# An attention, feed-forward and soft-mixture kernel on one core: weight conversion without a clamp, its additions on VectorE, some low parts on TensorE, and a maximum's reader put last

## The chip, the cores and the metric

One core of a Trainium2 chip runs the whole program. The metric is the device time of one execution in microseconds, the median of the runs. Engines are named as in the profile: PE is TensorE's matmuls, PEld its weight loads, DVE VectorE, ACT ScalarE, POOL GpSimd, SP SyncE, which issues the transfers.

## The reference

Three stages follow each other, all in float32; the two weights of the middle one come as float64 (random values divided by a square root), the others as float32.

```python
for t in range(S):                                   # B, H, S, D = 4, 8, 768, 48
    cur = np.einsum('bhd,bhe->bhde', u[None] * kt, vt)
    y[:, :, t] = np.einsum('bhd,bhde->bhe', rt, state + cur)
    state = wt[:, :, :, None] * state + np.einsum('bhd,bhe->bhde', kt, vt)
...
h = x @ w_in                                         # 3072 x 384 by 384 x 2048
g = h * (1.0 / (1.0 + np.exp(-1.702 * h)))
x2 = g @ w_out                                       # 2048 x 384
...
logits = x2 @ phi                                    # 32 slots, 8 experts x 4
d = softmax of logits over the tokens; slot_input = d.T @ x2
slot_out[e] = np.maximum(slot_input[e] @ w1[e], 0) @ w2[e]      # F = 1024
out = (softmax of logits over the slots) @ slot_out
```

## The kernel before

**Work and tiles.** The 3072 tokens are six blocks u of 512, one for each 128 steps of the sequence; a block has four attention units of 128 tokens, one for each batch element b, so 24 units. A unit (`unit_nodes`, L519) works in two halves of 64 steps. VectorE forms the running products of the decay by two scans (`scan0` L552, `scan1` L566) with their ends between them (L557, L560), and multiplies r and k by them (`scale` L574). TensorE forms the products of k and r (`pa` L600) and turns k (`pk` L605); VectorE masks them (`msk` L612). TensorE then does half 0 and half 1 (`half` L652, L654), with VectorE's new state after each (`snew` L659). The bonus term, r times u times k summed over a head and multiplied by v, is formed beside it from a second copy of r, k and v in natural order, the tile `nat` (load L543): two multiplications (`ruk` L582, L583), a sum over each head (`qsum` L587), a multiplication of v by it (`qv` L590). `yev` (L662) adds both; TensorE turns the result (`xtr` L668), ScalarE takes the high part (`xhi` L679) and VectorE the low part (`xlo` L682) of the input of the next stage.

**The feed-forward stage** (`mm_nodes`, L730) needs its inputs as a high and a low fp32r part. For each block and each of 16 weight groups f it does nine matmuls of h (L746), two gelu evictions on ScalarE (L750, L754), their difference on VectorE (`glo` L758), and nine matmuls into x (L766 to L768). Block 1 is done in two halves of 256 tokens, the others in one of 512.

**The conversion of the weights** (`conv_nodes`, L468) happens once per group f while block 0 runs. A group is 128x768 float64 values, loaded as pairs of 32-bit words (L477). ScalarE takes the absolute value of the high words into `cq` (L482) and shifts the low words (L483); VectorE clamps (`c1a` L486), shifts and masks (`c1b` L490) and adds the sign (`c1c` L494); GpSimd or VectorE adds the shifted low words as integers (`c2` L498; all 16 on GpSimd before); ScalarE rounds to the high part (`c3` L501), and VectorE subtracts for the low part (`c4` L504). The clamp keeps exponents in a range that the shift can carry.

**The last stage** (`moe2_nodes`, L786 and on) accumulates logits and slot inputs block by block with a running maximum (L840, L836, L844, L848), and after block 5 does the experts (L1100, L1142) and the output (L1161, L1182).

**A check of the range** of the decay products is made near 500 us: `inside0` (L1018 to L1020) on VectorE forms a column of flags, `inside1` (L1023) reduces it over the partitions on GpSimd, `inside2` (L1027) reads the result on VectorE, and the last instructions of the program (L1030, L1206) branch to a general path (not taken here) by it.

**The order.** `Plan` (L67) is a list scheduler that runs when the kernel is built. Every step is a node with an engine (or a table of engines with a cost each, as `C2E`), an assumed cost, its needs, a priority `pr` and the buffers it takes. The plan walks through assumed time and gives each free engine the ready node of the lowest priority; the result is a fixed order on each engine, and an instruction that waits holds up all behind it on its engine. Priorities of the units, the conversion and the matmuls come from the constants `FIRST`, `PERIOD`, `CONV0`, `CONVD`, `ATT0`, `ATTD`; the first loads are ordered by `SOON`; `tend` is the assumed end of the matmuls of block 5. VectorE steps marked `port=True` and GpSimd steps are kept apart in the plan's time.

## Time and profile before

| what | value |
|---|---|
| median of 3 runs | 634.65 us (633.98 to 636.14) |
| the profiled execution | 633.73 us |
| its span in the trace | 631.9 us |
| granted clock of TensorE, mean | 0.99 |
| PE busy | 570.4 us, 90% of the span |
| VectorE busy | 431.6 us, 68% |
| ScalarE busy | 274.9 us, 44% |
| GpSimd busy | 90.3 us, 14% |

The profiled execution's time is 1.8 us above its span: what lies around the first and the last instruction. All sums are made against the profiled execution. The shares are of the whole span, and its stages have different limits: the first 66.8 us go by until the first matmul of h, the feed-forward stage runs to about 584 us, and the experts and the output follow.

### The profile page before, as it was taken

What the parts mean: (1) busy time and instruction counts of PE and PEld (TensorE: products, weight loads), DVE (VectorE), ACT (ScalarE), POOL (GpSimd) and SP (SyncE); (2) the same over time, 40 slices, a digit from 0 to 9 for tenths busy, and PEclk for the clock granted to TensorE, in tenths of its full rate; (3) what the DMA queues carried; (4) which work ended last, traced back from release to release, by engine and by line L of the source; (5) the groups of instructions that cost most, each with busy time, mean ns of one, the idle gap of its engine ahead of it and who ended that gap; (6) DMA issues with size and microseconds to landing.
All of it is one profiled execution on the core that took longest, in us unless ns stands there. A gap on an engine that the chain in (4) does not pass through costs nothing.

```text
span 631.9 us, 12380 instructions
## 1 busy us (share of the span) xinstructions
PE 570.4 (90%) x5092; PEld 462.7 (73%) x5092; DVE 431.6 (68%) x830; ACT 274.9 (44%) x524; POOL 90.3 (14%) x83
## 2 busy tenths in 40 slices
...
GB/s 294 233 240 209 140 104 158 215 150 76 115 114 114 107 108 113 7 107 74 91 76 101 55 110 77 101 113 28 74 39 1 95 357 147 153 229 249 306 152 219
DMA packets 29475, 86.08 MB, mean 136 GB/s; under 512 B 3040, under 2 KB 12384, under 8 KB 29408
## 3 DMA queue, kind: packets, MB, share of 16 engines
q1 hardware_dynamic: 29408, 85.19, 41.0%
...
HBM read 80.46 MB, written 4.72 MB: 135 GB/s over the span
## 4 chain that ended last, share of the span: by engine, by line
PE 74%; DVE 14%; issue 4%; DMA 3%; ACT 2%; POOL 1%; SPq 0%; ACTq 0%; DVEq 0%
PE h L746 28%; PE x L766 10%; PE x L767 9%; PE x L768 9%; PE y L652 5%; DMA raw<-in_wf_dram 2%; PE y L654 2%; PE aps L600 2%; PE so L1142 2%; PE eh L1100 2%; PE xps L668 1%; DVE glgh L758 1%; DVE at L574 1%; DVE at L552 1%; PE fo L1182 1%
## 5 line engine op out<-in xcount | busy, mean ns | idle before, releaser
L746 PE MATMUL h<-xth,w 128*128 128x512 f32 (+1 forms) x672 | 205.9, 371 | 3.2 <-ACT w L501 2.0
L750 ACT ACTIVATE ghgh<-h 128x512 fp32r<-128x512 f32 (+1 forms) x112 | 60.0, 537 | 231.7 <-PE h L746 171.0
L746 PEld LDWEIGHTS h<-xth,w 128*128 128x128 f32 x672 | 123.2, 191 | 25.8 <-ACT w L501 2.1
L766 PE MATMUL x<-ghgh,w 128*128 128x512 f32 (+1 forms) x336 | 125.7, 374 | 0.0
L746 PE MATMUL h<-xtl,w 128*128 128x512 f32 (+1 forms) x336 | 122.3, 364 | 0.5 <-DVE xtl L682 0.5
L767 PE MATMUL x<-glgh,w 128*128 128x512 f32 (+1 forms) x336 | 121.7, 362 | 0.6 <-DVE glgh L758 0.4
L768 PE MATMUL x<-ghgh,w 128*128 128x512 f32 (+1 forms) x336 | 121.4, 361 | 0.0
L758 DVE TENSOR_TENSOR glgh<-g,ghgh 128x512 fp32r<-128x512 f32 (+1 forms) x112 | 73.5, 657 | 55.4 <-ACT g L754 54.2
L766 PEld LDWEIGHTS x<-ghgh,w 128*128 128x128 f32 x336 | 63.9, 190 | 11.2 <-issue 0.6
L652 PEld LDWEIGHTS y<-vs,st 128*64 128x64 f32 (+2 forms) x768 | 55.0, 151 | 22.8 <-issue 13.2
L767 PEld LDWEIGHTS x<-glgh,w 128*128 128x128 f32 x336 | 63.9, 190 | 10.5 <-DVE glgh L758 1.9
L746 PEld LDWEIGHTS h<-xtl,w 128*128 128x128 f32 x336 | 64.2, 191 | 9.9 <-DVE xtl L682 1.4
L768 PEld LDWEIGHTS x<-ghgh,w 128*128 128x128 f32 x336 | 63.7, 190 | 9.6
L652 PE MATMUL y<-vs,st 128*64 128x48 f32 (+2 forms) x768 | 61.7, 238 | 9.0 <-DVE ind L551 4.7
L754 ACT ACTIVATE g<-h 128x512 f32<-128x512 f32 (+1 forms) x112 | 59.8, 534 | 4.8 <-DVE glgh L758 3.9
L654 PE MATMUL y<-vs,st 128*48 128x48 f32 (+2 forms) x704 | 50.1, 229 | 0.2 <-ACT st L622 0.2
L659 DVE TENSOR_TENSOR vs<-y,fl 48x384 f32<-48x384 f32 x44 | 24.4, 555 | 37.1 <-PE y L654 36.4
L498 POOL TENSOR_TENSOR cq<-cq,raw 128x768 int32<-128x768 int32 x16 | 32.1, 2008 | 112.2 <-DVE cq L494 52.2
L582 POOL TENSOR_TENSOR nat<-nat 128x384 f32<-128x384 f32 x16 | 16.2, 1012 | 217.4 <-DMA nat<-in_nat_dram 133.7
L654 PEld LDWEIGHTS y<-vs,st 128*48 128x48 f32 (+2 forms) x704 | 44.1, 133 | 0.8 <-ACT st L622 0.6
L600 PE MATMUL aps<-at 48*64 48x64 f32 x768 | 23.6, 239 | 20.5 <-DVE at L574 13.0
L612 DVE TENSOR_TENSOR st<-aps,mask 64x256 f32<-64x256 f32 (+1 forms) x80 | 37.8, 472 | 4.7 <-PE aps L600 3.7
(143 smaller groups left out, 695.8 us busy)
## 6 DMA issues: line engine op xcount, KB each, us to landing
...
```

The costliest lines, as they stand in the source:

```text
L498: onto[e].tensor_tensor(a, a, words(0), op=ALU.add)
L600: pe.matmul(ab[p if four else 0][vl:vh, col:col + CH], t_[a_][lo:hi, 1, 4 * g + h], t_[a_][lo:hi, 0, 4 * g + h], start=True, stop=True)
L612: ve.tensor_tensor(S[0][vl:vh, p, n * g:n * g + n, 0:CH], t_[kap[p if four else 0]][al:ah, 0:n * CH].rearrange("p (h t) -> p h t", h=n), m ...
L652: pe.matmul(yps[vl:vh, cols], S[0][0:k1, p, h, 0:CH], rhs, start=True, stop=True)
L654: pe.matmul(sps[ol:oh, cols], S[0][0:k1, p, h, CH:ROWS], rhs, start=True, stop=True)
L746: pe.matmul(h[:, :wd], a, b, start=(k == 0), stop=(k == len(seq) - 1))
L750: ac.activation(t_[kgh][0], t_[kh][:, :wd], AF.Gelu_apprx_sigmoid)
L754: ac.activation(t_[kg], t_[kh][:, :wd], AF.Gelu_apprx_sigmoid)
L758: ve.tensor_tensor(gl, t_[kg], gh.bitcast(F32), op=ALU.subtract)
L766: pe.matmul(o, whi, gh, start=(f == 0), stop=False)
L767: pe.matmul(o, whi, gl, start=False, stop=False)
L768: pe.matmul(o, wlo, gh, start=False, stop=(f == NF - 1))
```

## The change

- **Conversion.** The clamp `c1a` is gone. The absolute value is taken with a scale of 2 to the −112, which moves the exponent by itself, and ScalarE sums it into a column of `wchk` for each group; `inside0` tests the 16 sums in three more VectorE instructions. `c1b` only shifts.
- **Addition.** `C2E` names VectorE alone, so all 16 additions `c2` are VectorE's (L512 of the new kernel).
- **Low parts.** For groups 0 to 3 (`C4PE = 4`) the low part is formed on TensorE: for each half of 384 columns a product with the identity and one with its negative (`less`, made once on ScalarE) add up in a PSUM bank (L523, L524), and ScalarE copies the bank (L527).
- **Bonus sums of block 0** (`UQ = 1`). Its four units load only v in natural order. VectorE multiplies r and k in the transposed layout (`prk` L621), and 16 one-column matmuls with u as the moving column (`qpe` L627) sum them into free columns of the bank of `pk`; `qv` (L634) reads them there. u is loaded a second time, transposed, by two transfers (L474); its wide copy `ubt` is loaded later.
- **Order.** `SOON`, `FIRST`, `CONV0`, `CONVD` and `ATTD` change.
- **The reader.** GpSimd's all-reduce gets a priority of its own and a cost of 11.5, and its reader `inside2` (L1081) comes at `tend + 40`, after `nsi`.

```diff
-C2E = {"DVE": 1.16, "POOL": 1.95}
+C4PE = 4
+UQ = 1
+C2E = {"DVE": 0.96}
-SOON = "w0 r0 c0 n0 u w1 r1 v0 n1 v1 w2 r2 n2 v2 c1 w3 r3 n3 v3"
-FIRST, SECOND, PERIOD, LAG, AHEAD = 42.0, 150.0, 82.0, 4.2, 74.0
-CONV0, CONVD, CONVL = 0.0, 6.0, 16.0
-ATT0, ATTD = 3.0, 6.0
+SOON = "w0 r0 n0 c0 w1 r1 v0 n1 v1 w2 r2 n2 v2 c1 w3 r3 n3 v3"
+FIRST, SECOND, PERIOD, LAG, AHEAD = 30.0, 150.0, 82.0, 4.2, 74.0
+CONV0, CONVD, CONVL = 6.0, 5.0, 16.0
+ATT0, ATTD = 3.0, 3.0
...
+    def ld_u():
+        for lo, hi in ((CH, ROWS), (0, DH)):
+            sy.dma_start(ut[lo:hi], ub[0:1].rearrange("o (h d) -> d (o h)", h=NH))
...
-            ac.activation(t_[cq], words(1).bitcast(F32), AF.Abs)
+            ac.activation(t_[cq], words(1).bitcast(F32), AF.Abs, scale=2.0 ** -112, accum_out=wchk[:, f:f + 1])
...
-        def c1a():
-            ve.tensor_scalar(t_[cq], t_[cq], W_TINY, W_HUGE, op0=ALU.max, op1=ALU.min)
...
-            ve.tensor_scalar(a, a, 3, 0x3FFFFFF8, op0=ALU.logical_shift_left, op1=ALU.bitwise_and)
+            ve.tensor_scalar(a, a, 3, None, op0=ALU.logical_shift_left)
...
+        def c4p(z):
+            b, cols = bank(f"c4_{f}_{z}"), slice(z * DM, (z + 1) * DM)
+            pe.matmul(b[:, :DM], ident, t_[cq][:, cols], start=True, stop=False)
+            pe.matmul(b[:, :DM], t_["less"][:, 0, 0:P], wt[f][:, 0, cols], start=False, stop=True)
+        def c4a(z):
+            ac.activation(wt[f][:, 1, z * DM:(z + 1) * DM], t_[f"c4_{f}_{z}"][:, :DM], AF.Copy)
...
+            if few:
+                sy.dma_start(t_[n_][:, 2], nat[i, :, 2])
+            else:
+                sy.dma_start(t_[n_], nat[i])
...
+        def prk():
+            t = t_[a_][0:ROWS]
+            ve.tensor_tensor(rk(), t[:, 0], t[:, 1, :, ::-1], op=ALU.mult)
+        def qpe():
+            for h in range(NH):
+                for p in range(2):
+                    (lo, hi), (vl, vh) = RNG[p], VROW[p]
+                    pe.matmul(t_[kkp][vl:vh, 4 * ROWS + h:4 * ROWS + h + 1], rk()[lo:hi, h], ut[lo:hi, h:h + 1], start=True, stop=True)
...
+        ve.tensor_scalar(wchk, wchk, W_MOST, -1.0, op0=ALU.is_lt, op1=ALU.mult)
+        ve.tensor_reduce(t_["cm"][:, 2:3], wchk, axis=AX.X, op=ALU.max)
+        ve.tensor_tensor(t_["cm"][:, 0:1], t_["cm"][:, 0:1], t_["cm"][:, 2:3], op=ALU.max)
...
-    n = nin = N("DVE", 0.35, inside0, limits + [nep], tend - 70)
-    n = N("POOL", 0.57, inside1, [n], tend - 29)
-    nok = N("DVE", 0.1, inside2, [n], tend - 28)
+    n = nin = N("DVE", 0.75, inside0, limits + [nep], tend - 70)
+    nout = N("POOL", 11.5, inside1, [n], tend - 70)
...
+    nok = N("DVE", 0.1, inside2, [nout, nsi], tend + 40)
```

How the order of the instructions moves, at three places. The rows are those of the programs as built, in the order in which an engine takes them: line, operation, what it writes and reads, shape.

First, VectorE from the first `scale` (L574) of unit 0 on, before:

```order
L574 TENSOR_TENSOR at0_116<-at0_116 112x1024
L486 TENSOR_SCALAR cq0_140<-cq0_140 128x768
L490 TENSOR_SCALAR cq0_140<-cq0_140 128x768
L582 TENSOR_TENSOR nat0_133<-nat0_133 128x384
L583 TENSOR_TENSOR nat0_133<-nat0_133,ubt_90 128x384
L494 SCALAR_TENSOR_TENSOR cq0_140<-raw0_121,cq0_140 128x768
L612 TENSOR_TENSOR st0_96<-aps0_0_151,mask_79 64x8x64 x2
L587 TENSOR_REDUCE q0_209<-nat0_133 128x8
L590 TENSOR_TENSOR nat0_133<-nat0_133,q0_209 128x384
L659 TENSOR_TENSOR vs0_92<-y0_0_192,fl0_135 48x384
L551 MEMSET ind_91 112x8
L552 SCALAR_TENSOR_TENSOR at1_145<-at1_145,ind_91 112x512
```

and from the first `prk` (L621) of the changed kernel on, where `scale` is L604, the mask L656 and the scans L582 and L596:

```order
L621 TENSOR_TENSOR nat0_123<-at0_116 112x512
L504 TENSOR_SCALAR cq0_146<-cq0_146 128x768
L604 TENSOR_TENSOR at0_116<-at0_116 112x1024
L508 SCALAR_TENSOR_TENSOR cq0_146<-raw0_132,cq0_146 128x768
L581 MEMSET ind_91 112x8
L582 SCALAR_TENSOR_TENSOR at1_143<-at1_143,ind_91 112x512
L621 TENSOR_TENSOR nat1_151<-at1_143 112x512
L512 ISA cq0_146<-raw0_132,cq0_146 128x1536
L656 TENSOR_TENSOR st0_96<-aps0_0_165,mask_79 64x8x64
L587 TENSOR_TENSOR fl1_220<-at1_143 112x8
L656 TENSOR_TENSOR st0_96<-aps0_0_165,mask_79 64x8x64
L590 RECIPROCAL ind_91<-fl1_220 112x8
```

The clamp, the multiplications of `nat0` and the low part of group 0 are gone from this place; the scan of unit 1 and its `prk` stand before the masks of unit 0, and the addition (L512, 1536 elements in its listing) between them.

Second, TensorE between half 0 and half 1 of unit 0 (the results go to `y0_0`, the new state of half 1 to `y1_0`), before:

```order
L654 MATMUL y0_0_192<-vs0_92,st0_96 48x48
L652 MATMUL y0_0_192<-vs0_92,st0_96 64x48
L654 MATMUL y0_0_192<-vs0_92,st0_96 48x48
L652 MATMUL y0_0_192<-vs0_92,st0_96 64x48
L654 MATMUL y1_0_220<-vs0_92,st0_96 48x48
L652 MATMUL y0_0_192<-vs0_92,st0_96 64x48
L654 MATMUL y1_0_220<-vs0_92,st0_96 48x48
```

and now, where L696 and L698 are the matmuls of a half:

```order
L696 MATMUL y0_0_223<-vs0_92,st0_96 64x48
L698 MATMUL y0_0_223<-vs0_92,st0_96 48x48
L696 MATMUL y0_0_223<-vs0_92,st0_96 64x48
L698 MATMUL y0_0_223<-vs0_92,st0_96 48x48
L523 MATMUL c4_0_0_246<-cq0_146,ident_78 128x384
L524 MATMUL c4_0_0_246<-w0_145,less_121 128x384
L523 MATMUL c4_0_1_251<-cq0_146,ident_78 128x384
L524 MATMUL c4_0_1_251<-w0_145,less_121 128x384
L696 MATMUL y0_0_223<-vs0_92,st0_96 64x48
L698 MATMUL y1_0_263<-vs0_92,st0_96 48x48
L696 MATMUL y0_0_223<-vs0_92,st0_96 64x48
```

Before, half 1 followed half 0 directly; now the four products for the low part of group 0 (L523, L524) stand between them.

Third, VectorE at the check near 500 us, before, with the reader L1027 ahead of the running maximum (L840, L844) of block 4:

```order
L1018 MEMSET cm_5295 128x2
L1019 TENSOR_SCALAR rz_89<-rz_89 112x24
L1020 TENSOR_REDUCE cm_5295<-rz_89 112x1
L1027 TENSOR_SCALAR outside_5317<-cm_5295 128x1
L840 TENSOR_REDUCE mb4_5328<-lg4_5304 128x1
L844 TENSOR_SCALAR mrun0_83<-mb4_5328,mrun1_84 128x1
L819 COPY x2g_1405<-x2t4_0_5322 128x384
```

and now, where the maximum is L891 and L895:

```order
L1069 MEMSET cm_5363 128x3
L1070 TENSOR_SCALAR rz_89<-rz_89 112x24
L1071 TENSOR_REDUCE cm_5363<-rz_89 112x1
L1072 TENSOR_SCALAR mx_88<-mx_88 128x16
L1073 TENSOR_REDUCE cm_5363<-mx_88 128x1
L1074 TENSOR_TENSOR cm_5363<-cm_5363 128x1
L891 TENSOR_REDUCE mb4_5397<-lg4_5375 128x1
L895 TENSOR_SCALAR mrun0_83<-mb4_5397,mrun1_84 128x1
L870 COPY x2g_1313<-x2t4_0_5391 128x384
```

The reader, now L1081, is found after the slot inputs (L1059) and the first steps of block 5's softmax (L904, L905):

```order
L1059 TENSOR_TENSOR scrB_5370<-sp_5981,rz_89 128x24x4
L904 TENSOR_REDUCE rm5_5988<-ln5_5959 128x4
L905 TENSOR_TENSOR lc_1320<-ln5_5959,rm5_5988 128x128
L1081 TENSOR_SCALAR outside_6004<-cm_5363 128x1
L921 TENSOR_REDUCE zr5_6007<-lc_1320 128x4
```

The reader left the place directly behind the flags; three more instructions on flags (L1072 to L1074) stand there. On GpSimd the order of the all-reduce and its neighbours is the same in both.

## Rows read from the trace of the kernel before

**Rows 1.** The page: busy time of each engine, share of the span, instructions.
```profile
PE 570.4 (90%) x5092; PEld 462.7 (73%) x5092; DVE 431.6 (68%) x830; ACT 274.9 (44%) x524; POOL 90.3 (14%) x83
```

**Rows 2.** Windows: stretch, its length, busy PE, PEld, DVE, ACT, POOL, PEclk, DMA share, GB/s.
```profile
0.00:66.80 66.80, 31.11 (x412) 26.32 (x412) 61.70 (x105) 31.23 (x56) 13.77 (x16) 1.00 0.75 243
66.80:100.60 33.80, 33.76 (x135) 27.27 (x135) 28.32 (x38) 22.44 (x34) 9.43 (x5) 1.00 0.33 111
100.60:180.70 80.10, 74.07 (x794) 61.23 (x793) 71.83 (x125) 49.75 (x95) 17.85 (x13) 1.00 0.46 148
180.70:500.00 319.30, 318.17 (x2910) 264.41 (x2910) 238.88 (x488) 126.10 (x250) 47.00 (x45) 1.00 0.24 76
500.00:520.00 20.00, 15.14 (x89) 11.73 (x88) 6.61 (x21) 9.34 (x17) 1.78 (x5) 0.91 0.87 333
```

**Rows 3.** Waits of PE, 66.8 to 180.7: us in total, times, longest.
```profile
PE aps L600 <- ACT g L754: 2.6, 2, 1.4
PE h L746 <- ACT w L501: 2.0, 1, 2.0
```

**Rows 4.** Chain of waits, longest pieces: start, us, what.
```profile
66.84 9.39 PE h L746 x27
...
502.64 9.52 issue
```

**Rows 5.** Timeline, 500.9 to 514.8: start, us, engine, instruction, idle before it.
```profile
502.45 0.18 DVE L1020 TENSOR_REDUCE cm<-rz 112x1 f32<-112x24 f32 x1
...
507.76 0.82 PE L815 MATMUL x2t<-ident,x2t 128*128 128x128 f32 x6
512.16 0.38 POOL L1023 PARTITION_ALL_REDUCE cm<-cm  x1 [10.45 <-issue]
512.57 0.15 DVE L1027 TENSOR_SCALAR outside<-cm 128x1 int32<-128x1 f32 x1 [9.94 <-POOL cm L1023]
...
512.95 0.28 ACT L836 ACTIVATE lt<-lg 128x128 f32<-128x128 f32 x1 [7.58 <-DVE mb L840]
...
513.28 0.42 PE L848 MATMUL ln<-ident,lt 128*128 128x128 f32 x1 [4.71 <-ACT lt L836]
```

**Rows 6.** Lines of DVE, 0 to 160: form, count | busy, mean ns | idle before.
```profile
L494 DVE SCALAR_TENSOR_TENSOR cq<-raw,cq 128x768 int32<-128x768 int32 x16 | 15.2, 950 | 0.0
L504 DVE TENSOR_TENSOR w<-cq,w 128x768 fp32r<-128x768 f32 x16 | 15.1, 942 | 1.0 <-ACT w L501 1.0
L486 DVE TENSOR_SCALAR cq<-cq 128x768 f32<-128x768 f32 x16 | 13.4, 835 | 4.4 <-ACT cq L482 4.2
...
L574 DVE TENSOR_TENSOR at<-at 112x1024 f32<-112x1024 f32 x8 | 9.7, 1218 | 0.0
...
L612 DVE TENSOR_TENSOR st<-aps,mask 64x512 f32<-64x512 f32 x14 | 9.6, 685 | 2.7 <-PE aps L600 2.5
L490 DVE TENSOR_SCALAR cq<-cq 128x768 int32<-128x768 int32 x16 | 8.8, 553 | 0.0
...
L583 DVE TENSOR_TENSOR nat<-nat,ubt 128x384 f32<-128x384 f32 x8 | 6.0, 754 | 0.3
L590 DVE TENSOR_TENSOR nat<-nat,q 128x384 f32<-128x384 f32 x8 | 5.8, 723 | 0.1
...
L582 DVE TENSOR_TENSOR nat<-nat 128x384 f32<-128x384 f32 x8 | 4.3, 543 | 0.0
```

**Rows 7.** Line L498: count, ns least/median/most, first and last start.
```profile
L498 POOL TENSOR_TENSOR cq<-cq,raw x16: 1817/1914/2727, 14.7 to 147.1; 128x768 int32<-128x768 int32 x16
```

**Rows 8.** Timeline of DVE, 14.5 to 16, while L498 runs on POOL from 14.73.
```profile
15.04 1.93 DVE L590 TENSOR_TENSOR nat<-nat,q 128x384 f32<-128x384 f32 x1
```

**Rows 9.** Lines of PE, 600 to 632, shapes apart.
```profile
L1161 PE MATMUL ss<-sb,sel 128*128 128x192 f32 x8 | 1.8, 342 | 0.0
```

**Rows 10.** Line L679 on ACT: ns least/median/most.
```profile
L679 ACT ACTIVATE xth<-xps x24: 482/490/493, 22.6 to 500.2; 128x384 fp32r<-128x384 f32 x24
```

**Rows 11.** The page: DMA queue, packets, MB, share of 16 engines.
```profile
q1 hardware_dynamic: 29408, 85.19, 41.0%
```

More of the change, by code (lines that the diff above doesn't have):

```diff
@@ L456, in soon, with minus @@
         return keys.index(key) - 100.0 if key in keys else pr
-    lub = [N("DMA", 0.6, lambda: sy.dma_start(ubt, ub), pr=soon("u", 0.0))]
+    lub = [N("DMA", 0.6, lambda: sy.dma_start(ubt, ub), pr=30.0)]
     nst = [N("POOL", 1.49, lambda i=i: zeros(i), pr=-1 + i) for i in range(2)]
     nst += [N("ACT", 0.83, lambda i=i: eyes(i), [nst[i]], pr=-1 + i) for i in range(2)]
+    def minus():
+        t_["less"] = mp.tile([P, KC, T], F32R, tag="xtl", name="less", bufs=2)
+        ac.activation(t_["less"][:, 0, 0:P], ident, AF.Copy, scale=-1.0)
+    nless = N("ACT", act(P), minus, pr=5, take=[("xl", "less")])
+    def ld_u():
+        for lo, hi in ((CH, ROWS), (0, DH)):
+            sy.dma_start(ut[lo:hi], ub[0:1].rearrange("o (h d) -> d (o h)", h=NH))
+    lut = N("DMA", 0.3, ld_u, pr=-97.5)
     lphi = N("DMA", 0.2, lambda: sy.dma_start(phit, phi), pr=40)
@@ L512, in conv_nodes @@
         n = N("ACT", act(2 * DM), c3, [n], pr, use=[cq, wk])
-        conv[f] = N("DVE", dve(2 * DM), c4, [n], pr, use=[cq, wk], port=True)
+        if f < C4PE:
+            m = [N("PE", 1.3, lambda z=z: c4p(z), [n, nless], pr, take=[("ps", f"c4_{f}_{z}")], use=[cq, wk, "less"]) for z in range(2)]
+            m = [N("ACT", act(DM), lambda z=z: c4a(z), [m[z]], pr, use=[wk, f"c4_{f}_{z}"]) for z in range(2)]
+            conv[f] = N("X", 0.0, lambda: None, m, pr)
+        else:
+            conv[f] = N("DVE", dve(2 * DM), c4, [n], pr, use=[cq, wk], port=True)
     limits, grp_last = [], {}
@@ L688, in unit_nodes @@
         lv = N("DMA", 0.55, ld_v, [h.get("h0"), h.get("h1")], soon(f"v{i}", pr(2) - 6))
-        ln = N("DMA", 1.64, ld_n, pr=soon(f"n{i}", pr(1) - 5), take=[("nat", n_)])
+        few = u < UQ
+        ln = N("DMA", 0.55 if few else 1.64, ld_n, pr=soon(f"n{i}", pr(1) - 5), take=[("nat", n_)])
         def psum(key):
@@ L702, in unit_nodes @@
         rc = [N("ACT", act(512), lambda p=p: rcp(p), [r0, sd, kt.get((0, 1)) if p else None], pr(3.2 + p), use=[a_, s_]) if u or p else None for p in range(2)]
-        p0 = N(RUKE[u > 1], 0, ruk, [ln] + ([lub[0]] if i < 2 else []), pr(1.5), use=[n_], port=True)
+        if not few:
+            p0 = N(RUKE[u > 1], 0, ruk, [ln, lub[0]], pr(1.5), use=[n_], port=True)
         ta = N("PE", 0.8 if four else 1.08, pa, [a1, r0], pr(2), take=[x for k in kap for x in psum(k)], use=[a_])
@@ L712, in unit_nodes @@
         k1 = N("DVE", 2 * dve(256) if four else dve(512), lambda: msk(1), [ta, kt.get((1, 1))], pr(3.5), use=[kap[-1], s_])
-        qs = N("DVE", dve(DM), qsum, [p0], pr(3.6), take=[("q", q_)], use=[n_])
-        qm = N(QVE[u > 1], 0, qv, [qs], pr(3.8), use=[n_, q_], port=True)
+        if few:
+            qs = N("PE", 1.0, qpe, [tk, p0, lut], pr(3.2), use=[kkp, n_])
+            qm = N("DVE", dve(DM), lambda: qv("DVE"), [qs], pr(3.8), use=[n_, kkp])
+        else:
+            qs = N("DVE", dve(DM), qsum, [p0], pr(3.6), take=[("q", q_)], use=[n_])
+            qm = N(QVE[u > 1], 0, qv, [qs], pr(3.8), use=[n_, q_], port=True)
         h0 = N("PE", 1.06, lambda: half(0), [k0, rc[0], lv, h.get("s1")] + ke0, pr(4), take=psum(ky0), use=[s_])
```

18 lines of the change are left out of this document (11 added, 7 removed).

## The prediction

> **What bounds the kernel now.** I read the page first, then the windows, then the waits of one engine in one window, then the chain. The page gives one core, a span of 631.9 us and TensorE busy for 570.4 of it [rows 1]. That share is an average over stages with different limits, so the windows come next. Up to 66.8 us VectorE is busy for 61.70 and TensorE for 31.11: the head, which prepares block 0 and converts the first weights, is bound by VectorE. From 66.8 to 100.6 TensorE is full (33.76 of 33.80). From 100.6 to 180.7 it has 74.07 of 80.10, VectorE 71.83: the two share the limit. From 180.7 to 500 TensorE is full (318.17 of 319.30), and nothing that another engine saves there counts. From 500 to 520 there is a hole, 15.14 of 20, and the granted clock is 0.91 [rows 2].
>
> The waits tell what the idle time of 66.8 to 180.7 us is: TensorE waits 2.6 us for the gelu's eviction to free a bank, 2.0 for one converted weight (ScalarE's rounding at L501), and smaller things [rows 3]; the windows put all of it at 6.1. The chain gives the start of the first matmul of h, 66.84, and a piece of 9.52 us at 502.64 in which nothing is computed, which it calls issue [rows 4].
>
> That piece is the hole. VectorE's reduction (L1020) ends at 502.63, GpSimd's all-reduce (L1023) starts only at 512.16 and takes 0.38, and VectorE, whose next instruction reads its result (L1027), stands still for 9.94 us. Behind it in VectorE's order stands the maximum L840, ScalarE's L836 waits 7.58 for that, and TensorE waits 4.71 for ScalarE [rows 5].
>
> **The change, part by part.** The sum is made against the profiled execution, 633.73 us; the median of the runs, 634.65, is 0.9 above it.
>
> *Clamp, additions, low parts.* Per weight group VectorE loses the clamp L486 (0.835 us in the mean; its like without a neighbour on GpSimd, L490, takes 0.553) and gains the addition, which took GpSimd 1.914 in the median (L498) [rows 6, 7]. No row shows an integer addition on VectorE. The nearest is L494: the same 768 words of both operands, the same stride in the raw ones, 0.950. The other end follows from the order listing, where the instruction has 128x1536 elements, two for each word: L612 takes 0.685 for 512 elements and L574 1.218 for 1024, so 1.04 ns for each further one, and 1536 would take 1.75 [rows 6]. I take 0.95, since the traffic is that of L494 and since the planner's table, whose other entries stand near the rows (1.95 for the addition on GpSimd), has 0.96; 0.95 and 1.75 are the bounds.
>
> [...]
>
> Four groups lose the subtraction L504 on VectorE (0.942 each) [rows 6]. It becomes two products for each half on TensorE and a copy on ScalarE. An fp32 product of 192 columns takes 0.342 as recorded, ends included [rows 9]; 384 columns are then at most 0.7, an fp32r one of 384 at most the same: at most 2.8 us a group, 11 us in all, before the first h, in a stretch with 35 us of idle TensorE [rows 2]. So nothing, unless they stand in the way of a half. They stand between half 0 and half 1 of unit 0 (second order piece). They need the rounding on ScalarE, about 1 us after the addition; half 1 needs eight further VectorE rows, two masks of 0.685, a scan of 1.2 and others, some 4 us. The products fit between. The copies are 8 x 0.490, as L679 [rows 10], on ScalarE, which is busy for 31 of 66.8.
>
> *Block 0.* Each of its four units drops L582, L583 (0.543 and 0.754) and L587, of the same 384 elements and priced as L582, for one multiply of 112x512, priced as the mask L612 of 512, 0.685 [rows 6]. The sums become 16 one-column products a unit. Even at the 0.342 of 192 columns the 64 of them would be 22 us, which with the 11 above still fits into 35; I put nothing on them.
>
> *Up to the first h.* The order listings, cut at the low part of unit 3, give 6, 6, 6 and 5 instructions of L486, L490, L494 and L504 before, and 0, 5, 5 and 0 after. Undisturbed (L486 as L490, L583 as L582), the change takes away 6 x 0.553 + 0.553 + 0.950 + 5 x 0.942 + 4 x 3 x 0.543 = 16.0 us and adds 5 x 0.95 + 4 x 0.685 + 0.2 (one more reciprocal) = 7.7, so 8.3 less on the engine that bounds. GpSimd's additions, beside which an instruction of VectorE runs longer (one L590 took 1.93 where its mean is 0.723 [rows 6, 8]), are gone as well, some 2 us here. The bounds for the first h are therefore 0 and −10.3. I take **−5.5**, two thirds of 8.3: an engine that has less to do waits more, and it waits 5.1 us in this stretch already. The DMA order is the other reason: 384 KB less for each of the four units, but ahead of the first raw weights come two loads of u in pieces of 4 bytes, 768 of them. A packet takes 141 ns in the mean (41.0% of 16 engines' 631.9 us, over 29408) [rows 11], so at most 6.8 us over 16 engines, and nothing if pieces of 4 bytes are cheap. I put 0.5 on it, in the third that I leave out.
>
> *After the first h.* Over the 16 groups VectorE gets 16 x (0.95 − 0.835) = +1.8 for addition against clamp, less the disturbance of others (L583 and L590 by 8 x (0.754 − 0.543) and 8 x (0.723 − 0.543), 3.1 us). The supply of weights and the turns of VectorE make TensorE's 6.1 us of waits; they can go as a whole or not at all (0 and −6.1). VectorE has 13.8 us idle in these 114 already and gets some 1.3 more, and the weights arrive earlier; so I take **−4**.
>
> *The reader last.* The all-reduce stays where it is (third order piece), but VectorE's next is the maximum L840, now L891, which needs only logits that TensorE formed before the hole. The last thing TensorE does ahead of it ends at 508.58 [rows 5]; by then the maximum and ScalarE's L836 can be done. So the 4.71 us go, and a little of what the clock costs: 0.09 of 15.14 us is 1.4 at most. Bounds: −3.8 (if some other hand-off of 0.9, as ScalarE's after this one, is next) and −6.1. I take **−5.0**. What is late next would be the new reader, but it stands after all gelu work, some 60 us later, when the all-reduce is long done.
>
> *Added checks.* Three small VectorE instructions at 0.18 us at most, as L1020 [rows 5]: **+0.4**, and 16 reads of an accumulator on ScalarE beside other work.
>
> Sum: −5.5 − 4 − 5.0 + 0.4 = −14.1, so 633.7 − 14.1 = **619.6 us**.
>
> **The rivals.** *Dear addition (1.75 us).* Up to the first h five additions cost 4.0 more, leaving −1.5 of the first term; after it eleven cost 8.8 more, which eats the second term. With the hole gone: 633.7 − 1.5 − 5.0 + 0.4 = 627.6. For it: 1536 elements. Against: the traffic of L494. Chance 0.2.
>
> *The columns of u hold the head.* If the 4-byte pieces cost the 6.8 us of their upper bound ahead of the first raw weights, the first term becomes −5.5 + 6.3 = +0.8: 625.9. For it: DMA engines are 0.75 busy up to 66.8 [rows 2]. Against: 48 rows of 8 elements are little data. Chance 0.1.
>
> *The wait stays.* If something else in VectorE's or ScalarE's order still needs the all-reduce, or its start moves along, the third term is 0: 624.6. The order piece speaks against it. Chance 0.05.
>
> *Slower.* VectorE takes for the addition what GpSimd takes. L498 has 1.82 at the least and 2.73 at the most [rows 7]. With a price x, VectorE has 16 (x − 0.835) more, less 3.8 for L504, 4.6 for block 0 and 3.1 for disturbance; if nothing covers it, all of it falls on the time. With the 4.6 of the hole won, the kernel gets slower from x = 1.85; at 2.3 it is +11.9 − 4.6, that is 641. Against: every 768-element row of VectorE lies under 0.96 undisturbed, and VectorE still idles some 24 us up to 250. Chance 0.06.
>
> **How the numbers follow.** My forecast has 0.59. Its own range is 611 to 627: all bounds at their best give 633.7 − 10.3 − 6.1 − 6.1 + 0.4 = 611.6; at their worst, with a hole only partly filled, 630. The range to 629 takes in the first three rivals and leaves out the slower side and the unluckiest sums. A measurement of this kernel tells 0.3%, 1.9 us, from no change. Faster takes the forecast, the two rivals around 625 and most of the dear addition: 0.88. Same 0.06: the dear addition with nothing covered (VectorE then +3.1, the hole −4.6). Slower 0.06.
>
> **What would show it.** First h at about 61 us instead of 66.8; L512 of the new kernel at 0.95 us (1.75 shows the first rival, 1.9 and more the last); no instruction of 384 elements at 1.9; TensorE's idle time in the 114 us after it down from 6.1 to under 3; no wait of 9.9 us on VectorE near 500 and no stop of TensorE there; products of L523 and L524 inside TensorE's idle time. A first h that comes no earlier, with VectorE waiting for raw weights, shows the second rival. I am wrong if the first h comes earlier and the end does not: then TensorE, full from 180 us on, took the gain back in waits between.

## The result and the profile after

The changed kernel takes 614.57 us in the median (611.57 to 618.76, 4 runs) beside 635.39 for the kernel before on the same chip: a ratio of 0.9673, with a 95% interval of 0.9601 to 0.9745. A second set, listed below as `a_ctrl`, gives 615.37 (611.39 to 617.05, 6 runs) and 0.9669 (0.9626 to 0.9711). The profiled execution took 616.53, 17.2 us less than the 633.73 of before. That is near the forecast sum of −14.1, but the terms came out otherwise than their working had it.

The page of the changed kernel, busy time of each engine (before: [rows 1]):

```profile
PE 577.8 (94%) x5244; PEld 467.4 (76%) x5244; DVE 415.2 (68%) x822; ACT 279.5 (45%) x548; POOL 58.0 (9%) x67
```

Its windows, with the columns of [rows 2], cut at its own stages (63.5 is just ahead of its first matmul of h, 63.52):

```profile
0.00:63.50 63.50, 42.19 (x564) 32.87 (x565) 50.53 (x90) 32.52 (x65) 4.02 (x11) 0.84 0.68 210
63.50:93.00 29.50, 28.86 (x128) 23.66 (x127) 28.09 (x41) 24.07 (x43) 0.00 (x0) 1.00 0.54 173
93.00:140.00 47.00, 47.00 (x401) 38.17 (x400) 43.40 (x67) 32.57 (x60) 0.11 (x1) 1.00 0.47 150
140.00:190.00 50.00, 49.99 (x683) 46.74 (x681) 45.88 (x102) 26.57 (x63) 10.75 (x9) 1.00 0.44 140
190.00:487.00 297.00, 296.26 (x2637) 243.57 (x2636) 216.67 (x451) 118.78 (x230) 41.47 (x44) 1.00 0.24 74
487.00:505.00 18.00, 17.61 (x113) 13.40 (x112) 9.16 (x29) 10.98 (x20) 1.16 (x2) 1.00 0.97 371
```

Three things stand in them. The head, the stretch up to the first matmul of h, is 3.3 us shorter, and VectorE, busy for 61.70 of 66.80 before, is now busy for 50.53 of 63.50: it no longer bounds the head. TensorE is full from 93 us on, where 6.03 of 80.10 us were idle. And the hole near 500 us is gone, 17.61 of 18 where it was 15.14 of 20.

To say where time went, I cut each trace at TensorE's own landmarks: the first matmul of h, the 28th, the first of block 2, the first of block 5, the last, and the last matmul of the program. The 1008 matmuls of h are the same in all kernels. Work can stand on either side of a landmark: between the 27th and the 28th matmul of h before has two groups of nine matmuls into x, 4.3 us, and the changed kernel one, 2.3 us. So 2 us between the second and the third stretch are order; their sum compares. In us:

| stretch | before | after | difference |
|---|---|---|---|
| start to the first h | 66.84 | 63.52 | −3.3 |
| first 27 matmuls of h | 13.31 | 9.16 | −4.2 |
| to the first h of block 2 | 167.88 | 161.15 | −6.7 |
| blocks 2 to 4 | 254.01 | 253.87 | −0.1 |
| block 5 | 73.71 | 67.74 | −6.0 |
| last h to the last matmul | 44.94 | 48.00 | +3.1 |
| sum | 620.68 | 603.44 | −17.2 |

The third stretch is the change's largest gain, and the last a loss that the forecast did not have.

The price on which the first rival hung is in the lines of VectorE, 0 to 160 us (line, form, count | busy, mean ns | idle before):

```profile
L512 DVE CUSTOM_DVE_ANT_0 cq<-raw,cq 128x1536 uint16<-128x1536 uint16 x16 | 15.2, 953 | 0.1
L508 DVE SCALAR_TENSOR_TENSOR cq<-raw,cq 128x768 int32<-128x768 int32 x16 | 15.2, 950 | 0.1
```

The addition takes 0.953 us over 1536 two-byte elements, as its neighbour of 768 words does, and not the 1.75 of the other bound: 0.62 ns for an element, where each further element of L574 over L612 took 1.04 [rows 6]. A rule of the Trainium skill ("VectorE: DVE Perf Modes", section "Mode 2×_1P") lets two 2-byte values pass in a cycle where they are adjacent and aligned. Within each pair of the raw operand they are, and the 0.953 agrees with it; whether this custom instruction ran in that mode no run here shows.

The hole is closed in the way the forecast had it. The timeline of the changed kernel near 488 us; columns as in [rows 5]:

```profile
488.20 0.17 DVE L1072 TENSOR_SCALAR mx<-mx 128x16 f32<-128x16 f32 x1
488.39 0.17 DVE L1073 TENSOR_REDUCE cm<-mx 128x1 f32<-128x16 f32 x1
488.60 0.16 DVE L1074 TENSOR_TENSOR cm<-cm 128x1 f32<-128x1 f32 x1
...
490.75 0.29 DVE L891 TENSOR_REDUCE mb<-lg 128x1 f32<-128x128 f32 x1 [2.00 <-PE lg L884]
...
494.06 0.27 PE L899 MATMUL ln<-ident,lt 128*128 128x128 f32 x1
```

VectorE goes from the flags (three more instructions, 0.50 us) to the maximum, which waits for TensorE's logits alone. The transpose of the same logits (L899, before L848 with its 4.71 us of waiting) has no wait. The all-reduce itself still starts late, and its reader runs much later without a wait:

```profile
498.82 0.80 POOL L1077 PARTITION_ALL_REDUCE cm<-cm  x1 [11.46 <-DVE zr L923]
567.43 0.14 DVE L1081 TENSOR_SCALAR outside<-cm 128x1 int32<-128x1 f32 x1
```

### The profile page after: what moved, and what is told of

Its sections match the earlier page's. It is cut to its first block, busy times and chain, and to the rows that moved or that the text cites. A ratio compares the mean times of both kernels' runs of the same rounds, so it can differ in the third digit from the quotient of the medians.

```text
span 614.7 us, 12682 instructions
## 1 busy us (share of the span) xinstructions
PE 577.8 (94%) x5244; PEld 467.4 (76%) x5244; DVE 415.2 (68%) x822; ACT 279.5 (45%) x548; POOL 58.0 (9%) x67
## 4 chain that ended last, share of the span: by engine, by line
PE 88%; DVE 4%; DMA 3%; ACT 1%; issue 1%; SPq 1%; ACTq 0%; DVEq 0%
PE h L797 33%; PE x L817 12%; PE x L818 11%; PE x L819 11%; PE y L696 6%; PE aps L644 3%; PE y L698 2%; PE eh L1154 2%; PE so L1196 2%; DMA at<-in_aw_dram 2%; PE x2t L866 1%; PE xps L712 1%; PE fo L1236 1%; PE pp L936 1%; DMA raw<-in_wf_dram 1%
## 5 line engine op out<-in xcount | busy, mean ns | idle before, releaser
L797 PE MATMUL h<-xth,w 128*128 128x512 f32 (+1 forms) x672 | 203.7, 367 | 0.2
L797 PEld LDWEIGHTS h<-xth,w 128*128 128x128 f32 x672 | 122.0, 189 | 21.8 <-PE y L698 1.9
L797 PE MATMUL h<-xtl,w 128*128 128x512 f32 (+1 forms) x336 | 121.2, 361 | 1.1 <-DVE xtl L726 1.1
L809 DVE TENSOR_TENSOR glgh<-g,ghgh 128x512 fp32r<-128x512 f32 (+1 forms) x112 | 71.4, 637 | 56.9 <-ACT g L805 55.6
L797 PEld LDWEIGHTS h<-xtl,w 128*128 128x128 f32 x336 | 63.6, 189 | 10.4 <-DVE xtl L726 2.1
L818 PEld LDWEIGHTS x<-glgh,w 128*128 128x128 f32 x336 | 63.5, 189 | 9.3 <-DVE glgh L809 0.6
L696 PEld LDWEIGHTS y<-vs,st 128*64 128x64 f32 (+2 forms) x768 | 52.1, 145 | 17.5 <-issue 10.4
L696 PE MATMUL y<-vs,st 128*64 128x48 f32 (+2 forms) x768 | 58.6, 232 | 3.9 <-DVE vs L703 2.2
L698 PE MATMUL y<-vs,st 128*48 128x48 f32 (+2 forms) x704 | 48.1, 224 | 0.5 <-ACT st L666 0.4
L698 PEld LDWEIGHTS y<-vs,st 128*48 128x48 f32 (+2 forms) x704 | 42.2, 129 | 0.9 <-ACT st L666 0.8
L656 DVE TENSOR_TENSOR st<-aps,mask 64x256 f32<-64x256 f32 (+1 forms) x80 | 37.8, 473 | 6.0 <-PE aps L644 4.8
L612 POOL TENSOR_TENSOR nat<-nat 128x384 f32<-128x384 f32 x16 | 17.2, 1078 | 216.9 <-DMA nat<-in_nat_dram 109.0
L582 DVE TENSOR_TENSOR_SCAN at<-at,ind 112x512 f32<-112x512 f32 x24 | 29.4, 1225 | 11.0 <-DMA at<-in_aw_dram 10.4
L644 PE MATMUL aps<-at 48*64 48x64 f32 x768 | 22.0, 231 | 15.0 <-DVE at L604 15.0
```

The lines of the kernel that those rows point to most:

```text
L582: ve.tensor_tensor_scan(flat(t[:, 2]), flat(t[:, 2]), flat(ind), initial=0.0, op0=ALU.mult, op1=ALU.add)
L644: pe.matmul(ab[p if four else 0][vl:vh, col:col + CH], t_[a_][lo:hi, 1, 4 * g + h], t_[a_][lo:hi, 0, 4 * g + h], start=True, stop=True)
L656: ve.tensor_tensor(S[0][vl:vh, p, n * g:n * g + n, 0:CH], t_[kap[p if four else 0]][al:ah, 0:n * CH].rearrange("p (h t) -> p h t", h=n), m ...
L696: pe.matmul(yps[vl:vh, cols], S[0][0:k1, p, h, 0:CH], rhs, start=True, stop=True)
L698: pe.matmul(sps[ol:oh, cols], S[0][0:k1, p, h, CH:ROWS], rhs, start=True, stop=True)
L797: pe.matmul(h[:, :wd], a, b, start=(k == 0), stop=(k == len(seq) - 1))
```

## The experiments

All twelve were timed in five rounds beside the kernel before. "After" below is the changed kernel. A ratio is against before, with its 95% interval; the last six columns are the stretches of the table above, from each profiled execution. r1_reader and r4_ulater have the 4.3 us of before between the 27th and the 28th matmul of h, e11_uq0_fill has 3.0, and the others 2.3.

| kernel | median us | ratio (interval) | first h | 27 h | to block 2 | 2 to 4 | block 5 | tail |
|---|---|---|---|---|---|---|---|---|
| before | 633.9 to 635.6 | 1 | 66.84 | 13.31 | 167.88 | 254.01 | 73.71 | 44.94 |
| r1_reader | 627.04 | 0.9882 (0.9842 to 0.9921) | 66.29 | 12.83 | 169.29 | 253.69 | 67.70 | 47.99 |
| r6_conv | 627.74 | 0.9864 (0.982 to 0.9908) | 66.69 | 11.64 | 160.41 | 254.48 | 74.75 | 48.00 |
| e10_conv_reader | 620.85 | 0.9782 (0.9752 to 0.9812) | 66.68 | 11.40 | 161.21 | 254.23 | 67.73 | 44.91 |
| r3_c4dve | 623.16 | 0.9821 (0.9784 to 0.9858) | 64.77 | 10.76 | 167.02 | 254.25 | 67.70 | 44.94 |
| r2_pool | 620.46 | 0.9778 (0.9735 to 0.9822) | 62.47 | 8.66 | 166.19 | 254.28 | 67.74 | 44.94 |
| e9_oldc | 619.04 | 0.9734 (0.97 to 0.9768) | 66.75 | 10.04 | 161.98 | 253.93 | 67.74 | 46.61 |
| r5_uq0 | 615.05 | 0.9675 (0.9637 to 0.9713) | 63.80 | 8.18 | 162.83 | 253.85 | 67.75 | 46.63 |
| r4_ulater | 617.42 | 0.9723 (0.9688 to 0.9759) | 62.80 | 15.40 | 158.90 | 253.58 | 67.72 | 46.64 |
| a_ctrl (after) | 615.37 | 0.9669 (0.9626 to 0.9711) | 63.90 | 9.11 | 160.83 | 253.85 | 67.75 | 46.62 |
| r7_fill | 612.92 | 0.9644 (0.9606 to 0.9681) | 62.45 | 9.13 | 160.83 | 253.87 | 67.70 | 44.92 |
| e11_uq0_fill | 614.49 | 0.9672 (0.9647 to 0.9697) | 61.62 | 8.91 | 163.37 | 254.24 | 67.73 | 44.93 |
| e12_c4late | 620.73 | 0.978 (0.9751 to 0.981) | 64.92 | 8.17 | 167.97 | 254.13 | 67.70 | 44.94 |

r1 to r4, a_ctrl with r5 to r7, and e9 to e12 shared a chip each; across the three groups only the ratios compare. A single profile tells the first h to a microsecond or two at best: after, a_ctrl and r7_fill have the same order up to the tail and show 63.52, 63.90 and 62.45; r5_uq0 and e11_uq0_fill, alike in the same way, show 63.80 and 61.62.

In what follows, the slow level of TensorE's clock is 1.2 GHz and the other 2.4 GHz, a granted clock of 0.50 (r2_pool, 44 to 54 us) and of 1.00; a matmul of h with 512 columns then starts 0.43 us after the one before it instead of 0.23.

**r1_reader: the reader alone.**

```diff
 (kernel before)
-    n = N("POOL", 0.57, inside1, [n], tend - 29)
-    nok = N("DVE", 0.1, inside2, [n], tend - 28)
+    nout = N("POOL", 11.5, inside1, [n], tend - 70)
...
+    nok = N("DVE", 0.1, inside2, [nout, nsi], tend + 40)
     finish[0](nsi)
```

> The kernel before with nothing but the reader of the all-reduce moved last. Theory (the wait of 9.9 us on VectorE stopped TensorE for 4.7 us and cost it the clock besides): 5 to 6 us less than before, about 629 us, TensorE full from 500 to 520 us. Rival (something else needs the all-reduce, or the time is given back in the tail): within 1.9 us of before.

0.9882 of before, 6.9 us in the medians, a little more than the theory's 5 to 6. Block 5 takes 67.70 instead of 73.71, and the window that held the hole is full:

```profile
500.00:520.00 20.00, 19.61 (x123) 15.07 (x122) 9.42 (x27) 11.95 (x21) 1.79 (x5) 1.00 0.92 351
```

So one instruction in VectorE's order cost TensorE 6.0 us: 4.7 of waiting, and the rest in matmuls at the slow level behind it (granted clock 0.91 of this stretch in before [rows 2], 1.00 here).

**r6_conv: the conversion alone.** No clamp, the test by sums, additions on VectorE; everything else as before.

```diff
 (changed kernel)
-C4PE = 4
+C4PE = 0
-UQ = 1
+UQ = 0
...
-SOON = "w0 r0 n0 c0 w1 r1 v0 n1 v1 w2 r2 n2 v2 c1 w3 r3 n3 v3"
+SOON = "w0 r0 c0 n0 u w1 r1 v0 n1 v1 w2 r2 n2 v2 c1 w3 r3 n3 v3"
...
-FIRST, SECOND, PERIOD, LAG, AHEAD = 30.0, 150.0, 82.0, 4.2, 74.0
-CONV0, CONVD, CONVL = 6.0, 5.0, 16.0
-ATT0, ATTD = 3.0, 3.0
+FIRST, SECOND, PERIOD, LAG, AHEAD = 42.0, 150.0, 82.0, 4.2, 74.0
+CONV0, CONVD, CONVL = 0.0, 6.0, 16.0
+ATT0, ATTD = 3.0, 6.0
...
-    nout = N("POOL", 11.5, inside1, [n], tend - 70)
+    n = N("POOL", 0.57, inside1, [n], tend - 29)
+    nok = N("DVE", 0.1, inside2, [n], tend - 28)
...
-    nok = N("DVE", 0.1, inside2, [nout, nsi], tend + 40)
```

> The kernel before with the conversion's part alone: no clamp, the range test by sums, all 16 additions on VectorE; the low parts, the bonus sums, the order's constants and the reader as before. Theory (no GpSimd work beside VectorE, so its neighbours are no longer stretched, and a chain per group shorter by one hand-off and 1 us): 4 to 7 us faster than before, 627 to 630. Rival (VectorE gets 0.95 for 0.835 us per group and stays the bound): within 1.9 us of before.

0.9864, 7.9 us in the medians, a little over the upper end of the theory's gain. But the place is another than the forecast's: the first h comes at 66.69, no earlier than before, and all of the gain lies in the two stretches behind it, −9.1 in their sum. Two rows of its windows tell both sides:

```profile
0.00:66.70 66.70, 31.76 (x413) 26.57 (x413) 60.37 (x105) 33.50 (x64) 4.02 (x11) 1.00 0.73 243
...
78.30:238.70 160.40, 160.39 (x1697) 143.35 (x1695) 145.04 (x276) 90.81 (x192) 16.56 (x17) 1.00 0.39 121
```

In the head VectorE is about as busy as before, 60.37 us: what the dropped clamp and the freed neighbours give, the additions take. Behind the 27 matmuls TensorE has no idle time at all. This run drops the clamp and moves the additions in one, so it does not part the two.

**e10_conv_reader: both.** The edit of r6_conv, with the changed kernel's place of the reader kept.

> The kernel before with the conversion's part and the reader's place alone; low parts, bonus sums and constants as before. Theory (the two parts act at different places, one before 250 us and one at 500, and add up: 7.9 and 6.9 us): 14 to 15 us faster than before, 0.977 of it, so that all the rest of the change is worth some 6 us. Rival (what is won before 250 us is partly lost again): 10 us or less.

14.6 us in the medians (635.45 to 620.85), beside 7.9 + 6.9 = 14.8: the two add up, as they act 250 us apart. What is left to the low parts, the bonus sums, the constants and what they do together is the step from 0.978 to 0.967, some 7 us.

**r2_pool: the additions back on GpSimd.**

```diff
 (changed kernel)
-C2E = {"DVE": 0.96}
+C2E = {"POOL": 1.95}
```

> The changed kernel with all 16 additions back on GpSimd (1.9 us each beside VectorE), the rest of the change kept. Theory (VectorE is freed of what GpSimd's additions did to its neighbours, some 11 us, more than the 15 us of additions cost it where it waits anyhow): 4 to 8 us slower than the changed kernel, 618 to 622, VectorE instructions of 384 to 768 elements again stretched. Rival (after the change VectorE no longer bounds the head, it idles 13 of its 63.5 us there): within 2 us of the changed kernel, or faster.

The ratio is 0.9778 against 0.9669 of after: some 7 us slower, as the theory had it. Here too the head does not tell: its first h comes at 62.47, in the range of after's profiles. The loss is in the stretch to block 2, 166.19 for 161.15, in which TensorE waits again (waits of TensorE, 71 to 237 us, the longest; after has none there):

```profile
PE x L818 <- DVE glgh L809: 1.2, 2, 1.0
PE y L698 <- ACT st L666: 0.8, 1, 0.8
PE y L696 <- issue: 0.6, 1, 0.6
PE h L797 <- ACT w L515: 0.5, 1, 0.5
```

In its lines of 0 to 160 us VectorE's shift L504, which takes 0.546 in the changed kernel, is stretched to 0.741 beside GpSimd's additions:

```profile
L504 DVE TENSOR_SCALAR cq<-cq 128x768 int32<-128x768 int32 x16 | 11.9, 741 | 2.0 <-ACT cq L499 1.8
```

and, on GpSimd:

```profile
L512 POOL TENSOR_TENSOR cq<-cq,raw 128x768 int32<-128x768 int32 x16 | 34.0, 2123 | 96.7 <-DVE cq L508 60.5 <-DVE st L656 11.4 <-DVE fl L587 8.0
```

Taken form by form up to block 2, VectorE's other instructions run some 10 us longer here than in after. That is less than the 15.2 us of additions that VectorE is rid of, so the stretched neighbours alone do not account for the loss. An addition also takes 2.1 us here for 0.95 and needs a hand-off to another engine and back; how much each counts was not told apart.

**r3_c4dve: the low parts back on VectorE.**

```diff
 (changed kernel)
-C4PE = 4
+C4PE = 0
```

> The changed kernel with the low parts of groups 0 to 3 back on VectorE. Theory (the products keep TensorE at work in the head, so that the first 27 matmuls of h no longer run at the slow level, which is worth 3.3 us, and VectorE is spared 3.8 us): 4 to 7 us slower than the changed kernel, the first matmuls of h at 0.43 us again. Rival (the products stand in the way of the halves, and the slow level of the clock depends on other things): the first h earlier, the time 1 to 3 us less.

0.9821 against 0.9669: some 9.6 us slower by the ratios, 9.1 up to the last matmul of h in the profiles, and more than the theory's 4 to 7. The first matmuls of h come at 0.43 us again, as the theory had it, but the 27 take only 1.6 us more. The stretch to block 2 carries 5.9. TensorE's waits there (64.7 to 242 us, the three longest; total, times, longest) are back:

```profile
PE x L818 <- DVE glgh L809: 2.5, 3, 1.4
PE h L797 <- DVE st L656: 0.8, 1, 0.8
PE y L696 <- ACT st L666: 0.7, 1, 0.7
```

After has, from 63.5 to 180 us, the one row "PE h L797 <- DVE xtl L726: 0.6, 1, 0.6". The 3.8 us of VectorE's subtractions are thus worth more than their length. They do not do it alone: r6_conv has all its subtractions on VectorE, with the old constants and the old bonus sums, and no wait in a stretch of 160.41. My reading is that the units, groups and gelu differences of blocks 0 and 1 queue on VectorE in an order set for a VectorE without the subtractions; no run tries the old constants in this kernel.

**e9_oldc: the order's constants as before**, all parts kept.

```diff
 (changed kernel)
-SOON = "w0 r0 n0 c0 w1 r1 v0 n1 v1 w2 r2 n2 v2 c1 w3 r3 n3 v3"
+SOON = "w0 r0 c0 n0 u w1 r1 v0 n1 v1 w2 r2 n2 v2 c1 w3 r3 n3 v3"
...
-FIRST, SECOND, PERIOD, LAG, AHEAD = 30.0, 150.0, 82.0, 4.2, 74.0
-CONV0, CONVD, CONVL = 6.0, 5.0, 16.0
-ATT0, ATTD = 3.0, 3.0
+FIRST, SECOND, PERIOD, LAG, AHEAD = 42.0, 150.0, 82.0, 4.2, 74.0
+CONV0, CONVD, CONVL = 0.0, 6.0, 16.0
+ATT0, ATTD = 3.0, 6.0
```

> The changed kernel with the constants of the order (order of the first loads, begin and pitch of the units and of the conversion) as before, all other parts kept. Theory (the constants carry no part of their own; the low parts on TensorE and the additions on VectorE do): 614 to 618 us, within 0.5% of the changed kernel's 0.967 of before. Rival (the low parts on TensorE pay only when the units and groups are set closer): 4 to 8 us slower, TensorE idle between 75 and 240 us again.

0.9734 against 0.9669, some 4 us slower (the two intervals just overlap; in the profiles it is 5.0 up to the last matmul of h), with the first h at 66.75: that speaks against the theory and for the rival's amount, but not for its place, since TensorE does not idle later. This is the run that shows what shortens the head. VectorE's work is down to 54.19 us by 66.7, and yet the first h comes no earlier than before:

```profile
0.00:66.70 66.70, 45.01 (x564) 35.73 (x564) 54.19 (x94) 36.65 (x74) 4.02 (x11) 0.85 0.68 215
```

The table says the same throughout: the five profiles with the old constants have the first h at 66.3 to 66.8, whatever parts they have, and the nine with the new ones at 61.6 to 64.9.

**r5_uq0: block 0's bonus sums as before.**

```diff
 (changed kernel)
-UQ = 1
+UQ = 0
...
-    lub = [N("DMA", 0.6, lambda: sy.dma_start(ubt, ub), pr=30.0)]
+    lub = [N("DMA", 0.6, lambda: sy.dma_start(ubt, ub), pr=-96.5)]
...
-    lut = N("DMA", 0.3, ld_u, pr=-97.5)
+    lut = None
```

> The changed kernel with block 0's bonus sums formed as before (full natural loads, two multiplications and a sum on VectorE, u's wide copy loaded early, no transposed u). Theory (VectorE is relieved of 4 x 1.15 us in the head, and 1.5 MB less are loaded there): 2 to 4 us slower than the changed kernel. Rival (VectorE idles 13 of 63.5 us of the changed kernel's head, and waits 4.9 us there for ScalarE behind the one-column products, so the relief is not on the path): within 1.9 us or faster.

615.05 beside 615.37 on the same chip: no difference against a spread of 3 to 6 us between the runs of each, and the theory's 2 to 4 us are not seen, so the rival holds. The part takes 4.6 us (as the rows of before stand, disturbed ones too) from VectorE and 1.5 MB from the loads, and gives TensorE 64 one-column products in the head (128 records, 5.9 us) that stand in each unit's own chain.

**r4_ulater: u's columns behind the first raw weights.**

```diff
 (changed kernel)
-    lut = N("DMA", 0.3, ld_u, pr=-97.5)
+    lut = N("DMA", 0.3, ld_u, pr=-94.5)
```

> The changed kernel with the two transposed loads of u issued behind the first raw weights and the first r and k instead of ahead of them. Theory (the pieces of 4 bytes hold up the loads behind them; the first multiplication of r and k on VectorE waits 3.2 us for its load): the first prk starts at 9 to 10 us instead of 12.1, the first h comes 2 to 3 us earlier, the time is about 612. Rival (the head is set by hand-offs between VectorE, ScalarE and TensorE later on): the first prk earlier, the time the same.

The first prk starts at 8.77 us instead of 12.07, where it had waited in the changed kernel:

```profile
12.07 0.69 DVE L621 TENSOR_TENSOR nat<-at 112x512 f32<-112x512 f32 x1 [3.21 <-DMA at<-in_ark_dram]
```

Yet the first h, at 62.80, comes no earlier than in r7_fill (62.45), whose head is that of after, and the ratio, 0.9723, is no better than 0.9669. The rival holds. The 3.3 us won at the start are lost on the way to the first h. In this profile the stretch of the first 27 matmuls of h takes 15.40 us: 2.0 are order, one matmul waits 1.88 for a low part of the input on VectorE, and up to 68.3 us they come at 0.43.

**a_ctrl: the changed kernel again,** as the measure for this group.

> The changed kernel itself, as the measure for the others of this call: 612 to 617 us, or 0.967 to 0.974 of before.

615.37 and 0.9669, in line with the first set.

**r7_fill: six products in TensorE's waits ahead of the experts.**

```diff
 (changed kernel)
         def pp():
             b = bank(kpp)
+            if tail:
+                for _ in range(3):
+                    pe.matmul(b[:, :P], ident, ident, start=True, stop=True)
...
     def f6z():
-        pe.matmul(bank("sz")[:, 0:NSL], m2["prun"]()[:, DM:DM + 1].to_broadcast([P, P]), sm["mx"], start=True, stop=True)
+        b = bank("sz")
+        for _ in range(3):
+            pe.matmul(b[:, :P], ident, ident, start=True, stop=True)
+        pe.matmul(b[:, 0:NSL], m2["prun"]()[:, DM:DM + 1].to_broadcast([P, P]), sm["mx"], start=True, stop=True)
```

> The changed kernel with six products of the identity with itself (128x128, overwritten by the products that follow) in TensorE's waits between the last block and the experts. Theory (in the profile of the changed kernel the granted clock falls to 0.8 behind these waits, and 48 products of the experts take 7.9 instead of 5.4 us, in some executions and not in others): 1 to 3 us less than the changed kernel, with a narrower spread. Rival (the clock falls by what lies further back, or the products delay the chain): the same time within 1.9 us.

612.92 beside 615.37, with all six runs between 612.09 and 613.91 where after's lie between 611.39 and 617.05. The intervals of the two ratios overlap, so the gain of the median is likely, not shown. The spread of 1.8 us is what the theory asked for, but the products are not shown to be its cause: e11_uq0_fill and e12_c4late, which have them too, spread over 3.7 and 4.7 us, and r4_ulater without them over 2.6. What the products act on is seen in the windows. The changed kernel, from the logits of block 5 on:

```profile
559.60:567.00 7.40, 5.50 (x56) 3.69 (x54) 3.74 (x14) 2.76 (x8) 0.46 (x1) 0.90 0.88 329
567.00:580.00 13.00, 12.91 (x92) 4.38 (x96) 3.50 (x11) 2.61 (x5) 0.00 (x0) 0.80 0.51 196
```

and with the six products:

```profile
558.00:565.00 7.00, 6.54 (x69) 4.68 (x67) 3.70 (x14) 2.91 (x8) 0.46 (x1) 1.00 0.93 337
565.00:578.00 13.00, 12.86 (x112) 4.82 (x112) 3.62 (x12) 3.04 (x6) 0.00 (x0) 1.00 0.73 287
```

TensorE waits in the first of these windows for VectorE's small steps. At the end of these waits the granted clock falls in after's profile, and the 48 products of the experts take 7.93 us, where they take 5.36 with the six products:

```profile
567.09 7.93 PE L1154 MATMUL eh<-w,scrB 128*32 128x512 f32 x48 [0.40 <-issue]
565.14 5.36 PE L1160 MATMUL eh<-w,scrB 128*32 128x512 f32 x48 [0.41 <-issue]
```

The kernel before has the same waits and no fall in its profile; r1_reader and r6_conv have it. The windows of before:

```profile
579.90:586.90 7.00, 5.01 (x56) 3.21 (x55) 3.82 (x14) 2.79 (x8) 0.46 (x1) 1.00 0.92 332
586.90:599.90 13.00, 12.98 (x116) 4.87 (x120) 3.44 (x10) 3.15 (x6) 0.00 (x0) 1.00 0.74 289
```

Over the profiles without the six products the tail takes 44.9 us in four, 46.6 in four and 48.0 in three; with them it takes 44.9 in three of three, which four of eleven without them do as well.

**e11_uq0_fill: r5_uq0 and r7_fill together.**

> The changed kernel without the block 0 part (bonus sums as before) and with the six products in TensorE's waits ahead of the experts. Theory (the block 0 part is worth nothing, the products keep the clock): 612 to 613 us, as the changed kernel with the products alone (0.9644 of before). Rival (the block 0 part is worth 2 us that were hidden by the clock in the tail): 614 to 616.

0.9672 (614.49): the median lies in the rival's 614 to 616, but the lower end of the interval all but touches r7_fill's 0.9644, from another chip. The tail is 44.93 and the first h comes earliest of all, 61.62, but the stretch to block 2 takes 2.2 to 2.5 us more than in after. Block 0's part may be worth some 1.8 us by these ratios; this was not told apart from nothing.

**e12_c4late: the low parts' products later**, on top of r7_fill.

```diff
 (r7_fill)
-            m = [N("PE", 1.3, lambda z=z: c4p(z), [n, nless], pr, take=[("ps", f"c4_{f}_{z}")], use=[cq, wk, "less"]) for z in range(2)]
+            m = [N("PE", 1.3, lambda z=z: c4p(z), [n, nless], pr + 8.0, take=[("ps", f"c4_{f}_{z}")], use=[cq, wk, "less"]) for z in range(2)]
```

> The changed kernel with the six products in the tail, and with the low parts' products of groups 0 to 3 put behind the halves and transposes of block 0 where they stood ahead of them. Theory (in the head the chain runs through TensorE's products, 3.5 us for a group at the slow level, ahead of a half): the first h 1 to 3 us earlier, the time 610 to 612. Rival (the products then delay the first h, or the head is bound by VectorE anyhow): 612 to 615.

0.978, some 9 us slower than r7_fill, so both forecasts were wrong. The first h comes at 64.92 and the stretch to block 2 is 167.97 again. The products hold the tile `cq`, of which there are three, so a later product presumably holds up the next group's conversion; that was not tried by itself.

## Why the prediction was right, and where not

The time (614.6 in the median, 616.5 in the profiled execution, for 619.6) lies in the range of 611 to 627, and the sign came out as forecast. By its steps:

- **Addition, 0.95 us: right** (0.953). With it fall the dear addition and the slower side, whose point was 1.85.
- **Up to the first h, −5.5: measured −3.3, and the step behind it was wrong.** I counted 8.3 us less work on VectorE as the engine that bounds, and took two thirds. The work did go (VectorE 50.53 for 61.70), but r6_conv, e9_oldc and after show that the first h follows neither VectorE's sum nor the parts: 66.69, 66.75, 63.52. The constants, to which I gave no term, carry some 3 us (e9_oldc against after). My reading is that, once VectorE has gaps, a unit's chain through TensorE and ScalarE sets the head, and the constants decide how the units overlap; no run takes that chain apart.
- **Products on TensorE at no cost: wrong in the reason.** 35 us of idle TensorE is no cover when an engine takes its instructions in order: on the chain of e9_oldc, 10 to 67 us, the low parts' products are 18% of the time and the one-column products 11%. The price was too low as well. A record of [rows 9] is half an fp32 product (L1161 makes four products there, in eight records); against my bound of 2.8 us a group, the first three groups take 3.5 us each in the changed kernel, at the slow level of the clock, and the fourth some 2.2. TensorE is busy in the head for 42.19 us now. VectorE's multiplication by the bonus sums has a wait that it did not have before, put down to ScalarE's L666, which evicts the same bank behind the one-column products (waits of VectorE, 0 to 63.5):

```profile
DVE nat L634 <- ACT st L666: 4.9, 3, 2.8
```

  The lines of TensorE, 0 to 63.5 us, in the changed kernel:

```profile
L523 PE MATMUL c<-cq,ident 128*128 128x384 f32 x16 | 11.1, 791 | 0.6 <-DVE cq L512 0.6
L524 PE MATMUL c<-w,less 128*128 128x384 f32 x8 | 7.6, 948 | 0.0
...
L627 PE MATMUL kps<-mx,nat 48*64 48x1 f32 x128 | 5.9, 219 | 0.0
```

- **After the first h, −4: measured −10.9, mechanism right, size off.** The bounds went to −6.1, the visible waits, and those went to 0.6. What I left out: the first 27 matmuls of h themselves got some 2.9 us faster, since they no longer begin at the slow level (before, 27 in 9.39 [rows 4]; now 26 in 6.23):

```profile
64.56 6.23 PE h L797 x26
```

  Another 2.5 us I cannot name. To block 2 the additions' move alone is worth 5.0 us in the changed kernel (r2_pool); with the dropped clamp, in the kernel before, the two stretches are worth 9.1 (r6_conv).
- **Block 0 and its loads: no gain that r5_uq0 shows**; they are 3.6 of VectorE's 8.3 us in my working (four times 3 x 0.543 − 0.685, less 0.2).
- **The reader, −5.0: right**, −6.0 in block 5 including the three added instructions (0.50 for my 0.4); r1_reader shows the same 6.0 by itself.
- **The columns of u**: the second rival's mechanism is there, its price is not. In one window of the changed kernel, 4 to 5 us, the queue moves 780 packets for 0.13 MB:

```profile
q1 hardware_dynamic: 780, 0.13, 93.3%
```

  That is about a microsecond of DMA at full share, and with it a later first prk; r4_ulater shows that this is not what sets the first h.
- **The tail, +3.1: not foreseen.** It is the clock, and it changes between executions: the same kernel has a tail of 48.0 us in one profile and of 46.6 in the other.

Errors of opposite sign, +2.2 in the head and the tail's +3.1 against −6.9 behind the first h and −1.4 at the reader, are why the sum fell close; that it did is luck.

What stays open: why the low parts on TensorE are worth 9.6 us where VectorE's saved work is 3.8 (shown: the waits that return without them, and that r6_conv, with the old constants and bonus sums, has no such waits; not shown: which queue place makes each), whether the additions' move pays by the freed neighbours or by the shorter chain of a group, and what in an execution decides whether the first 27 matmuls of h and the tail run slow.
